# One sliding-window transformer block on one core: the unread output of the row maximum goes to two one-byte tiles in turn

## The chip, the core and the metric

The kernel runs on one core of a Trainium2 chip. The metric is the device time in microseconds (us) of that core, as the median of several executions. A core has five engines with an instruction queue each: TensorE (PE in the profile, with its weight loads as PEld), VectorE (DVE), ScalarE (ACT), GpSimd (POOL) and SyncE (SP, which only issues DMAs here). Each engine works through its own queue in order, and engines wait for each other, or for themselves, by semaphores.

## What is computed

The input is a sequence of 2048 tokens with 512 features. The reference, cut to what matters:

```python
qkv = layernorm(x) @ wqkv                       # 32 heads of 16
scores = einsum("bhqd,bhkd->bhqk", q, k) * (Dh ** -0.5)
mask = (i - j >= 0) & (i - j < 256)             # causal, window of 256
p = softmax(where(mask, scores, -1e9))
h = x + (p @ v) @ wo
g, u = layernorm(h) @ w_gate, layernorm(h) @ w_up
h2 = h + (sigmoid(g) * u) @ w_down              # inner width 1376
```

The softmax subtracts a maximum from each row of scores. That maximum is where the change lies.

## The kernel before, in words

Large products are made from pairs of 16-bit halves: a float32 operand is split into a high and a low part, and three products of parts are summed in PSUM (`mm3`, L399 to L402). The tokens go through in 8 blocks of 256 (`NB`, `B`). For a block, these pieces of work exist:

- `do_ln`: layer norm and transposition of two groups of 128 tokens.
- `do_qk` and `do_v`: the products for queries, keys and values (L402 on TensorE), whose results ScalarE and VectorE split and store (L656 on VectorE writes the low parts).
- `do_keys` and `do_queries`: DMAs that put keys and queries where TensorE reads them.
- `do_s` (L707 to L736): the scores in the layout with queries on partitions, only for the row maximum. For each of 8 groups of 4 heads there are 8 steps. A step makes 320 columns of scores with one or two matmuls (L735) into one of three PSUM tiles of the ring `s`, and queues a `row_max`.
- `row_max` (L713 to L724): one VectorE instruction (L720) that adds the mask to the scores and reduces them to the row maximum. The maximum goes to one column of the tile `mq`, through a second, short instruction that reads VectorE's accumulator. The elementwise sum has to be written somewhere too, and goes to the tile `junk`, which nobody reads. The PSUM tile is free for TensorE again when this has run (`plan.free("s", ...)`).
- `do_m`: turns 32 columns of maxima into two 16-bit halves and brings them, by DMA, into extra rows of the queries, so that the next product subtracts them.
- `do_st` (L756 to L803): the scores again, transposed (keys on partitions), with the maximum subtracted by the product itself; ScalarE takes the exponential out of PSUM (L765); GpSimd zeroes what lies outside of the window (L773, L778).
- `do_pv` (L807 to L839): probabilities times values (L826); ScalarE or VectorE takes the high half out of PSUM and VectorE the low half (L838).
- `do_o`, `do_wo`: transposition by DMA, division by the row sum (L868, L870), the output product and the residual sum.

After the last block the gated part runs in eight groups of 256 tokens: products with the gate and up weights (L1131), sigmoid and product (L1197 to L1215), and the down product (L1308, L1314). It needs no row maxima. The weights for it are prepared, by ScalarE, VectorE and GpSimd, while the attention blocks run.

The order of all this is fixed ahead of time. Each piece is a Python generator that says at every `yield` which engine it needs, for how long by the planner's estimate, and which earlier pieces must have been issued; a long list of numbers (`ORDER`) says which piece is issued next. So each engine's queue is the same list of instructions whatever the times on the chip are. For a row maximum the planner's estimate is (320 - c0) / 960 + 0.077, which is 0.41 us for 320 columns (L715). The semaphore waits are not written in the kernel; they are put in by the tile framework, from which tile each instruction reads and writes. The pool `swork`, in which `junk` lies, is opened with `reuse_waits="tile"` (L427): a new tile that takes the place of an older one waits until the instructions on that older one are done. `junk` has `bufs=1`, so each row maximum's `junk` takes the place of the one before it.

There are 8 blocks of 8 groups of 8 steps, so 512 row maxima; in the first block the four widths are 64, 128, 192 and 256 columns (`c0 = 256 - 64 * i`), 16 of each; the other 448 are over 320 columns.

Of the kernel before, what the change touches and what calls it, by code (L numbers as in the profile page):

```python
# [28 lines left out]
BF16 = mybir.dt.bfloat16  # L29
# [6 lines left out]
P = 128  # L36
# [296 lines left out]
def tile_block(ctx, tc, x, wqkv, wo, wg, wu, wd, out):  # L333
# [37 lines left out]
    def psum_tile(ring, shape, dt=F32):  # L371
        return psum.tile(shape, dt, name=ring + "p", tag=ring, bufs=RINGS[ring])
# [54 lines left out]
    swork = right.enter_context(tc.tile_pool(name="swork", bufs=2, side="right", reuse_waits="tile"))  # L427
# [279 lines left out]
    def do_s(b, g, prio):  # L707

        p, hf = g // 2, g // 4
        needs = [("queries", b, p), ("filled", 0)] + [("keys", a, hf) for a in (b, b - 1) if a >= 0]  # L710
        left = 8

        def row_max(ps, c0, x, i, e, n):  # L713
            nonlocal left
            e, = yield {DVE_: (320 - c0) / 960 + 0.077}, [e]  # L715
            plan.free("s", n, e)
            junk = swork.tile([P, 320], BF16, name="junk", bufs=1)
            if (b, hf) not in mq:
                mq[b, hf] = swork.tile([P, 8, 4], F32, name="mq", bufs=4)
            V.tensor_tensor_reduce(out=junk[:, c0:], in0=ps[:, c0:], in1=mask[:, c0:], scale=1.0, scalar=-3.0e38,  # L720
                                   op0=ALU.add, op1=ALU.max, accum_out=mq[b, hf][:, x, i:i + 1])
            left -= 1
            if left == 0:
                plan.mark(("s", b, g), e)  # L724

        for jj in range(2):
            j = 2 * (g % 2) + jj
            for i in range(4):
                c0 = 0 if b else 256 - 64 * i
                e, n = yield {PE_: (320 - c0) / 2400 + 0.006}, needs, ["s"], 0.75  # L730
                ps = psum_tile("s", [P, 320])
                q = SQ[b % 2][0:96, 4 * p + j, i].rearrange("p u t -> p (u t)")
                for a, k0, k1, col in ((b - 1, 64 * i, 256, 0), (b, 0, 64 * i + 64, 256 - 64 * i)):
                    if a >= 0:
                        PE.matmul(ps[:, col:col + k1 - k0], q, SK[0:96, (2 * a + hf) % 5, 4 * (p % 2) + j, k0:k1], start=True, stop=True)  # L735
                plan.add(prio + (4 * jj + i) / 8, row_max(ps, c0, 4 * (p % 2) + j, i, e, n))  # L736
# [745 lines left out]
```

## Time and profile before

| What | Value |
|---|---|
| time, three executions | 852.44, 852.42, 850.45 us; median 852.42 |
| profiled execution | 851.43 us, span of its instructions 849.6 us |
| TensorE busy | 765.7 us (90% of the span), 7014 matmuls |
| VectorE busy | 725.9 us (85%), 2052 instructions |
| ScalarE busy | 438.2 us (52%) |
| GpSimd busy | 277.9 us (33%) |
| mean granted TensorE clock | 0.97 |

The span runs from the first to the last instruction of the profiled execution; 1.8 us of its time lie around it. An engine is busy while at least one of its instructions is recorded as running. Records of one engine overlap: an instruction's record ends when its results are written, and the next one's can begin before that. So a record's length is not the pace at which such instructions follow each other; the pace is read from the starts. A row of the profile's groups names the line, the engine, the operation, the tiles written and read, the shape, the count, and then the busy time, the mean nanoseconds of one, and the engine's idle time ahead of them with what ended it. In the chain of waits and in the timelines the first two numbers of a row are the start, in us from the span's start, and the length.

### The profile page before, as it was taken

How to read it: one execution, taken by the hardware profiler on the slowest of the kernel's cores; microseconds unless marked ns; L12 is line 12 of the kernel's file. 1: busy time of each engine (PE TensorE's matmuls, PEld its weight loads, DVE VectorE, ACT ScalarE, POOL GpSimd, SP SyncE). 2: the span in 40 equal slices, each digit the busy share in tenths (PEclk: the TensorE clock that was granted, in tenths of full speed). 3: DMA queues.
4: the chain of work that ended last, by engine and by line, in shares of the span. 5: the costliest groups of instructions: out<-in, count | busy, mean ns of one | idle time of the engine just before them, and what ended most of it. 6: DMA issues, size and time to landing. Idle time of an engine off the chain costs nothing.

```text
span 849.6 us, 19062 instructions
## 1 busy us (share of the span) xinstructions
PE 765.7 (90%) x7014; PEld 509.9 (60%) x7014; DVE 725.9 (85%) x2052; ACT 438.2 (52%) x771; POOL 277.9 (33%) x342
## 2 busy tenths in 40 slices
PE   4788889999898899898999999658999999999997
PEld 3475557667666567566665555234756657567466
DVE  8988878888888889888987756999999888898983
ACT  5663656766568777767765766654221222112210
POOL 2632333424335354454445545655000000000000
PEclk9999988999999999999988999979999999999999
DMA  9585353374357459554965764974656458365536
GB/s 320 177 236 143 104 135 97 69 175 95 72 152 186 100 130 217 160 136 103 241 169 129 158 120 110 286 164 110 117 107 131 78 97 171 76 117 79 99 69 172
DMA packets 213326, 119.10 MB, mean 140 GB/s; under 512 B 176688, under 2 KB 185904, under 8 KB 213232
## 3 DMA queue, kind: packets, MB, share of 16 engines
q1 hardware_dynamic: 213232, 117.88, 59.1%
q8 instruction: 55, 0.90, 0.5%
q14 instruction: 39, 0.32, 0.1%
HBM read 43.65 MB, written 19.40 MB: 74 GB/s over the span
## 4 chain that ended last, share of the span: by engine, by line
PE 51%; DVE 32%; issue 7%; DMA 6%; ACT 1%; POOL 1%; DVEq 1%; SPq 0%; ACTq 0%; POOLq 0%
DVE junk L720 17%; PE sp L1131 12%; PE mmp L402 9%; PE mmp L1308 8%; PE pvp L826 6%; PE stp L1131 5%; PE sp L735 4%; PE pvp L1131 2%; PE stp L800 2%; PE stp L790 1%; DVE WD L951 1%; DMA x<-hl 1%; DVE sq L656 1%; PE mmp L1314 1%; DVE W L1021 1%
## 5 line engine op out<-in xcount | busy, mean ns | idle before, releaser
L720 DVE CUSTOM_DVE_ANT_0 junk<-sp,mask 128x320 bf16<-128x320 f32 (+4 forms) x512 | 239.5, 468 | 56.5 <-PE sp L735 9.3
L765 ACT ACTIVATE pa<-stp,kappa 128x512 f32<-128x512 f32 (+1 forms) x256 | 158.5, 645 | 81.5 <-PE stp L791 77.9
L735 PE MATMUL sp<-SK,SQ 96*128 96x256 f16 (+3 forms) x960 | 146.5, 237 | 37.3 <-DVE mq L720 29.1
L1131 PEld LDWEIGHTS <-x 128*128 128x128 f16 x1008 | 98.6, 98 | 105.9 <-issue 19.1
L1131 PE MATMUL sp<-W,x 128*128 128x512 f16 (+1 forms) x612 | 135.1, 361 | 14.2 <-DVE SQ L1154 10.5
L735 PEld LDWEIGHTS <-SQ 96*128 96x128 f16 x960 | 86.9, 99 | 86.9 <-issue 63.9
L402 PE MATMUL mmp<-xT,W 128*128 128x256 f16 x768 | 112.1, 276 | 4.9 <-DVE xT L357 2.2
L765 ACT ACTIVATE pb<-stp,kappa 128x512 f32<-128x512 f32 x128 | 85.6, 685 | 39.0 <-PE stp L800 38.1
L773 POOL TENSOR_SCALAR_AFFINE_SELECT pa<-pa 128x1024 f32<-128x1024 f32 x56 | 63.4, 1134 | 71.0 <-ACT pa L765 65.7
L402 PEld LDWEIGHTS <-W 128*128 128x128 f16 x768 | 70.3, 98 | 19.4 <-issue 5.0
L778 POOL TENSOR_SCALAR_AFFINE_SELECT pb<-pb 128x512 f32<-128x512 f32 x64 | 42.7, 667 | 71.4 <-ACT pb L765 64.2
L778 POOL TENSOR_SCALAR_AFFINE_SELECT pa<-pa 128x512 f32<-128x512 f32 x64 | 43.3, 677 | 65.3 <-ACT pa L765 65.3
L826 PE MATMUL pvp<-pa,VT 128*17 128x128 f32 (+1 forms) x1408 | 63.8, 312 | 0.6 <-DVE RH L838 0.6
L558 POOL TENSOR_TENSOR rs<-rs,nhalf 128x1 f32<-128x1 f32 x32 | 19.7, 619 | 131.5 <-DVE rs L555 131.2
L790 PE MATMUL stp<-SQ,SK 100*128 100x256 f16 x224 | 61.3, 278 | 0.0
L402 PE MATMUL mmp<-WO,oT 128*128 128x512 f16 x192 | 54.5, 405 | 5.5 <-DMA oT<-whl 5.3
L1131 PE MATMUL stp<-W,x 128*128 128x512 f16 (+1 forms) x264 | 58.2, 357 | 0.9 <-DVE SQ L359 0.6
L791 PE MATMUL stp<-SQ,SK 100*128 100x128 f16 x256 | 57.0, 223 | 0.2
L362 DVE TENSOR_TENSOR hr<-SQ,hr 128x512 f16<-128x512 f32 (+3 forms) x90 | 52.0, 588 | 2.4 <-ACT hr L355 1.6
L826 PEld LDWEIGHTS pvp<-pa,VT 128*17 128x17 f32 x1408 | 38.5, 99 | 24.7 <-issue 6.0
L800 PE MATMUL stp<-SQ,SK 100*128 100x256 f16 x256 | 50.5, 283 | 2.2 <-ACT pa L765 2.2
L1197 ACT ACTIVATE SQ<-sp,cg 128x512 f32<-128x512 f32 (+1 forms) x22 | 14.0, 638 | 73.2 <-PE sp L1131 73.2
(210 smaller groups left out, 1418.0 us busy)
## 6 DMA issues: line engine op xcount, KB each, us to landing
SQ<-sq SPq DMA_DIRECT2D x96, 128.0 KB
wr<-chunk SPq DMA_DIRECT2D x28, 256.0 KB
W<-wr SPq DMA_DIRECT2D x14, 512.0 KB
SK<-mem SPq DMA_DIRECT2D x16, 384.0 KB
chunk<-in_wd_dram SPq DMA_DIRECT2D x20, 256.0 KB
X<-in_x_dram SPq DMA_DIRECT2D x16, 256.0 KB
mem<-sk SPq DMA_DIRECT2D x8, 512.0 KB
out_dram<-X SPq DMA_DIRECT2D x16, 256.0 KB
```

What stands on the lines that cost most here:

```text
L402: PE.matmul(ps, a_of(a, k), b_of(b, k), start=(k == 0 and i == 0), stop=(k == n - 1 and i == 2))
L720: V.tensor_tensor_reduce(out=junk[:, c0:], in0=ps[:, c0:], in1=mask[:, c0:], scale=1.0, scalar=-3.0e38, op0=ALU.add, op1=ALU.max, accum_ou ...
L735: PE.matmul(ps[:, col:col + k1 - k0], q, SK[0:96, (2 * a + hf) % 5, 4 * (p % 2) + j, k0:k1], start=True, stop=True)
L765: S.activation(dst, a, AF.Exp, scale=kappa)
L773: G.affine_select(out=f, in_=f, pattern=[[0, 8], [-1, 128]], compare_op=ALU.is_gt, fill=0.0, base=0, channel_multiplier=1)
L778: G.affine_select(out=p, in_=p, pattern=[[0, 4], [1, 128]], compare_op=ALU.is_ge, fill=0.0, base=0, channel_multiplier=-1)
L790: PE.matmul(a[:, 128:384], ks(k0 + 1, g, j), qs(b, g, j, 0, 256), start=True, stop=True)
L791: PE.matmul(a[:, 384:512], ks(k0 + 3, g, j), qs(b, g, j, 128, 256), start=True, stop=True)
L800: PE.matmul(a[:, u, :], ks(k0 + 2, g, j + u), qs(b, g, j + u, 0, 256), start=True, stop=True)
L826: PE.matmul(ps[32 * j:32 * j + 17, u, q0:q1], VT[:, kt % 6, 8 * j + g, :], w[:, j, c:c + q1 - q0], start=first, stop=last, skip_group_chec ...
L1131: PE.matmul(ps, X2[p % 2][part][:, (a * COUNT[part] + at) * 2 + k, :], W[c][:, b, j, k, :], start=first and k == 0 and i == 0, stop=k == 1 ...
L1308: PE.matmul(ps, hT[p, c, r][:, a, half * kinds[c] + i, :], W["d"][2 * c + i][:, b, j, :], start=fresh and c == 0 and i == 0 and n == 0, st ...
```

## The change

The tile for the unread elementwise result becomes one byte wide per element in place of two, and there are two such tiles in turn in place of one. Two tiles of 320 bytes take as many bytes of a partition, 640, as the one tile of 320 bf16 elements did. The instruction, its inputs, its maximum and its place in VectorE's queue stay.

```diff
         def row_max(ps, c0, x, i, e, n):
             nonlocal left
             e, = yield {DVE_: (320 - c0) / 960 + 0.077}, [e]
             plan.free("s", n, e)
-            junk = swork.tile([P, 320], BF16, name="junk", bufs=1)
+            junk = swork.tile([P, 320], mybir.dt.uint8, name="junk", bufs=2)
             if (b, hf) not in mq:
                 mq[b, hf] = swork.tile([P, 8, 4], F32, name="mq", bufs=4)
             V.tensor_tensor_reduce(out=junk[:, c0:], in0=ps[:, c0:], in1=mask[:, c0:], scale=1.0, scalar=-3.0e38,
                                    op0=ALU.add, op1=ALU.max, accum_out=mq[b, hf][:, x, i:i + 1])
```

## The prediction

> **What bounds the kernel now.** I first cut the span where the row maxima begin and end, and read the busy time of each engine per stretch. The columns are the stretch and its length, then busy us and instruction count of PE, PEld, DVE, ACT and POOL, the granted clock, the DMA share and GB/s.
>
> ```profile
> core 0: us, PE busy (x) PEld busy (x) DVE busy (x) ACT busy (x) POOL busy (x), PEclk, DMA share, GB/s
> 0.00:45.40 45.40, 29.49 (x206) 20.24 (x207) 39.98 (x93) 27.48 (x54) 21.35 (x34) 0.96 0.76 252
> 45.40:483.20 437.80, 396.42 (x4446) 278.03 (x4445) 376.35 (x1316) 294.52 (x513) 186.52 (x229) 0.96 0.58 140
> 483.20:550.00 66.80, 58.41 (x515) 30.34 (x514) 47.35 (x85) 43.04 (x73) 35.30 (x39) 0.97 0.70 178
> 550.00:849.60 299.60, 281.35 (x1851) 181.27 (x1849) 262.27 (x563) 73.19 (x134) 34.71 (x41) 0.98 0.57 115
> ```
>
> Only the second stretch, 437.80 us long, holds row maxima, so only it can change directly. By busy time TensorE (396.42) stands ahead of VectorE (376.35). That is misleading, and the groups of this stretch show why:
>
> ```profile
> line engine op names shapes xcount | busy us, mean ns | idle before us <-releasers
> L720 DVE CUSTOM_DVE_ANT_0 junk<-sp,mask 128x320 bf16<-128x320 f32 (+4 forms) x512 | 239.5, 468 | 56.5 <-PE sp L735 9.3 <-PE stp L791 1.0
> L735 PE MATMUL sp<-SK,SQ 96*128 96x256 f16 (+3 forms) x958 | 146.3, 237 | 37.3 <-DVE mq L720 29.1
> L402 PE MATMUL mmp<-xT,W 128*128 128x256 f16 x638 | 95.3, 274 | 1.5 <-DVE sq L656 1.5
> L720 DVE DVE_READ_ACCUMULATOR2_ANT mq<- 128x1 f32 x512 | 42.2, 83 | 0.0
> ```
>
> VectorE is idle for 437.80 - 376.35 = 61.5 us of the stretch, and 56.5 of these lie directly before row maxima. TensorE accounts for only 9.3 + 1.0 us of them. The other 56.5 - 10.3 = 46.2 us have no releaser named. TensorE's largest idle time, 37.3 us before the score matmuls, is mostly (29.1) a wait for the row maximum. So here VectorE sets the pace, and part of its time goes to something that is neither work nor another engine. Its timeline shows what:
>
> ```profile
> start us, us, engine line op out<-in xcount [idle before <-releaser]
> 203.18 0.08 DVE L720 DVE_READ_ACCUMULATOR2_ANT mq<- 128x1 f32 x1
> 203.18 1.38 DVE L656 SCALAR_TENSOR_TENSOR sq<-mmp,sq 64x512 f16<-64x512 f32 x2
> 204.60 0.49 DVE L720 CUSTOM_DVE_ANT_0 junk<-sp,mask 128x320 bf16<-128x320 f32 x1
> 205.01 0.08 DVE L720 DVE_READ_ACCUMULATOR2_ANT mq<- 128x1 f32 x1
> 205.13 0.49 DVE L720 CUSTOM_DVE_ANT_0 junk<-sp,mask 128x320 bf16<-128x320 f32 x1
> 205.55 0.08 DVE L720 DVE_READ_ACCUMULATOR2_ANT mq<- 128x1 f32 x1
> 205.66 0.49 DVE L720 CUSTOM_DVE_ANT_0 junk<-sp,mask 128x320 bf16<-128x320 f32 x1
> 206.08 0.08 DVE L720 DVE_READ_ACCUMULATOR2_ANT mq<- 128x1 f32 x1
> 206.08 1.38 DVE L656 SCALAR_TENSOR_TENSOR sq<-mmp,sq 64x512 f16<-64x512 f32 x2
> 207.50 0.49 DVE L720 CUSTOM_DVE_ANT_0 junk<-sp,mask 128x320 bf16<-128x320 f32 x1
> 207.91 0.08 DVE L720 DVE_READ_ACCUMULATOR2_ANT mq<- 128x1 f32 x1
> 208.14 0.49 DVE L720 CUSTOM_DVE_ANT_0 junk<-sp,mask 128x320 bf16<-128x320 f32 x1
> ```
>
> Compare the starts. Behind the row maximum of 205.66 comes an L656 that touches no `junk`: it starts at 206.08, 0.42 us later, together with the accumulator read and before the row maximum's own record has ended. Behind the row maxima of 204.60, 205.13 and 207.50 comes another row maximum: 0.53, 0.53 and 0.64 us later, after the accumulator read has ended. The chain of waits has the 0.64 pair in pieces:
>
> ```profile
> 207.50 0.49 DVE junk L720
> 207.99 0.02 DVE mq L720
> 208.01 0.03 issue
> 208.04 0.02 DVEq L720
> 208.06 0.08 issue
> 208.14 0.49 DVE junk L720
> ```
>
> DVEq is VectorE's queue at work on an instruction that only waits. It can act once the accumulator read has ended (207.99 + 0.02), and the row maximum begins 0.13 us after that. I read the wait as VectorE's wait for itself. In the code the new `junk` takes the place of the last one (`bufs=1`), and the write into it must be behind the earlier write. The other output is no reason: the columns of `mq` are distinct, and the two L656 in one row (x2, 1.38 us together) write different parts of one tile directly behind each other without a gap.
>
> **The change part by part.**
>
> *Two tiles in turn.* The wait stays in the program but aims at the row maximum before the last. That one's accumulator read is over at the latest about 0.1 us into the last one (205.01 + 0.08 = 205.09 against the start at 205.13), so the wait passes while the last one runs. What a row maximum behind a row maximum then costs, no row shows, since all wait today. Bounds: with nothing left it follows after 0.42 us, as L656 does; if it has to let the accumulator read end, after 0.49 (205.01 + 0.08 - 204.60). I take 0.42, the pace of the row that stands in the same place.
>
> How many pairs? At 0.64 the idle time is 208.14 - (207.91 + 0.08) = 0.15, so the 46.2 us make about 46.2 / 0.15 = 308 pairs. Pairs at 0.53 have only some 0.03 idle each; they are left out of the count, and each would add 0.11. Per pair two things go: the 0.15 of idle time and the 0.083 of the accumulator read, which lies uncovered today. Together 46.2 + 308 x 0.083 = 46.2 + 25.6 = **71.8 us of VectorE time**. With 0.49 it is the 46.2 alone.
>
> *One byte per element.* No instruction of the trace writes single bytes, so its cost is bounded by rows on output width and on width of the tile.
>
> ```profile
> L359 DVE TENSOR_SCALAR SQ<-sp 128x512 f32<-128x512 f32 x11 | 7.6, 687 | 7.3 <-PE sp L1131 7.3
> L359 DVE TENSOR_SCALAR RH<-pvp 128x512 f16<-128x512 f32 x8 | 5.5, 686 | 5.5 <-PE pvp L826 5.5
> L720 DVE CUSTOM_DVE_ANT_0 junk<-sp,mask 128x320 bf16<-128x320 f32 x448 | 218.8, 488 | 50.3 <-PE sp L735 9.0 <-PE stp L791 1.0
> L720 DVE CUSTOM_DVE_ANT_0 junk<-sp,mask 128x64 bf16<-128x64 f32 x16 | 3.6, 223 | 1.6 <-PE sp L735 0.3
> ```
>
> From PSUM, four-byte and two-byte results take 687 and 686 ns: the width of the result does not count there. I take nothing, the value of these nearest rows. A row maximum costs (488 - 223) / 256 = 1.04 ns per element; that another 1.04 ns could be needed to place a byte is my bad end, and none of these rows points below nothing. The tiles take the bytes of the old one, so nothing else moves.
>
> *What VectorE's gain is worth.* If all else could follow, the stretch would shrink by 71.8 us. It can't quite. VectorE's busy time falls to 376.35 - 25.6 = 350.8, below TensorE's. Of TensorE's 396.42 part is only the tail of records, as this row of the chain shows beside L402's mean of 274 ns:
>
> ```profile
> 41.50 3.67 PE mmp L402 x33
> ```
>
> 33 matmuls in 3.67 us are 0.11 us each, so a record outlives the stream by some 0.16, once for each run of matmuls. TensorE's need is below 396 by an amount I can't read off; taken at face value it limits the gain to 437.8 - 396.4 = 41 us. So the ends are 41 and 72 us. Between them I go by the last stretch, without row maxima, where TensorE and VectorE feed each other in the same way: TensorE is busy 281.35 / 299.60 = 0.94 and VectorE 262.27 / 299.60 = 0.875 of it. VectorE's 350.8 at 0.94 makes 373 us (gain 65), at 0.875 401 us (gain 37). I take the middle, 387 us, a gain of **51 us**. That the queue order was laid out with 0.41 us per row maximum (L715), which is the new pace, speaks against the lower end. What is late next is TensorE, with the score matmuls in a queue between projections and `do_pv`; behind it the DMA transpositions and POOL's masking, which have the same lengths in less time. DMA is at 0.58 in the stretch and would be near 0.66.
>
> The other stretches keep their length and start earlier. Sum: 851.4 (this profiled execution; its span 849.6 and 1.8 around it) - 51 = 800.4. The median of the runs shown is 1.0 above the profiled execution, so I say **801 us**.
>
> **The rivals.**
>
> *A. Another engine or a DMA takes over early (slightly faster).* The row maxima come sooner, but TensorE has no scores ready, or the chain runs through transpositions and masks. For: TensorE's 396.4 busy us; the chain also passes DMAs and TensorE. Against: VectorE waits for TensorE before row maxima only 10.3 us in all. A gain of 5 to 20 us: some 840 us.
>
> *B. Single bytes are slow to write (slower).* Price: 1.04 ns more per element. The elements are 448 x 320 + 16 x (64 + 128 + 192 + 256) = 153,600, so 159 us more of VectorE, against 72 less: 852 + 159 - 72 = 939 us. It decides from 72 / 153.6 = 0.47 ns per element on, so from a record of 488 + 320 x 0.47 = 638 ns for 320 columns. Against: the equal 686 and 687. For: no row shows single bytes.
>
> *C. The wait is not `junk`'s, or taking it away frees nothing (the same).* The pace between row maxima might come from VectorE having to empty itself before the next such instruction. Then the gaps stay and the time is 852. Against: L656 starts 0.42 us after a row maximum. For: no row has two row maxima without a wait. The Trainium skill, "VectorE: DVE Perf Modes", section "The DRAIN you can't avoid", states such a rule: the next operation can't issue until the pipe is empty, and of eight copies with a semaphore after each and eight with one at the end it says that "the semaphore costs nothing extra here". By that rule the result is this rival's 852; the trace disagrees, with 0.42 us without and 0.53 to 0.64 with a wait behind equal instructions.
>
> **How the numbers follow.** Forecast (faster by 20 to 77 us, with the 0.49 case in it): 0.79. A: 0.07. B: 0.09. C: 0.05. So faster by over 0.3% 0.86, within 0.3% 0.05, slower by over 0.3% 0.09; 0.3% is about what a measurement of this kernel can tell from no change. The range: below, the whole 72 us and some 50 pairs at 0.53 on top (5 us), 775; above, 0.49 in place of 0.42 with its loss in coupling (46 x 51 / 72 = 33 us, so 819) and 13 us more of such loss, 832. It leaves out B, C and A, together 0.21.
>
> **What would show it.** Starts of row maxima in a row 0.42 us apart, and the unnamed idle time before L720 down from 46 to some few us (C: unchanged; the 0.49 case: the accumulator read still uncovered). A row maximum's record still near 488 ns (B: towards 820). The stretch of the row maxima some 387 us long, with VectorE's named waits for TensorE well over 10.3 us and TensorE's wait for the row maximum under 29.1; the last stretch still about 300 us. If the first two hold and the stretch is over 420 us, A is right and my share of 0.91 was wrong.

## The result and the profile after

The changed kernel takes 787.72 us (median of 4 executions, 786.26 to 790.29) against 852.18 us for the kernel before (median of 4): a ratio of 0.925, with a 95% interval of 0.922 to 0.928, so 64 us less. The profiled execution took 786.26 us, its span is 784.5 us.

First the same cut as before the change, with the stretch that holds the row maxima in the second row. The columns are the stretch and its length, busy us and count of PE, PEld, DVE, ACT and POOL, the granted clock, the DMA share and GB/s.

```profile
core 0: us, PE busy (x) PEld busy (x) DVE busy (x) ACT busy (x) POOL busy (x), PEclk, DMA share, GB/s
0.00:46.50 46.50, 29.54 (x206) 20.98 (x207) 40.05 (x92) 27.41 (x54) 21.51 (x34) 0.96 0.80 242
46.50:418.80 372.30, 361.93 (x4449) 268.37 (x4447) 351.30 (x1316) 289.72 (x514) 185.34 (x228) 1.00 0.71 165
418.80:490.00 71.20, 61.40 (x531) 31.34 (x529) 53.03 (x93) 46.59 (x81) 39.83 (x44) 0.98 0.75 193
490.00:784.50 294.50, 277.32 (x1835) 179.60 (x1833) 256.95 (x556) 69.38 (x126) 31.36 (x38) 0.99 0.56 111
```

The stretch went from 437.80 to 372.30 us, 65.5 us less. What lies behind it takes 71.2 + 294.5 = 365.7 us, against 66.8 + 299.6 = 366.4 before. So all of the gain is in the stretch. VectorE's busy time there fell from 376.35 to 351.30, and TensorE's busy share of the stretch rose from 0.91 to 361.93 / 372.30 = 0.97.

The groups of that stretch for the row maximum and the score matmuls (busy us, mean ns, then idle time before them by releaser):

```profile
L720 DVE CUSTOM_DVE_ANT_0 junk<-sp,mask 128x320 uint8<-128x320 f32 (+4 forms) x512 | 214.0, 464 | 12.1 <-PE sp L735 10.6
L735 PE MATMUL sp<-SK,SQ 96*128 96x256 f16 (+3 forms) x958 | 132.8, 232 | 5.8 <-DVE mq L720 4.0
```

The idle time before the row maxima is 12.1 us, of which 10.6 are waits for TensorE: 1.5 us have no releaser named, where there were 46.2. TensorE's wait for the row maximum fell from 29.1 to 4.0 us. VectorE's timeline shows the new pace:

```profile
start us, us, engine line op out<-in xcount [idle before <-releaser]
183.42 0.48 DVE L720 CUSTOM_DVE_ANT_0 junk<-sp,mask 128x320 uint8<-128x320 f32 x1
183.82 0.09 DVE L720 DVE_READ_ACCUMULATOR2_ANT mq<- 128x1 f32 x1
183.82 0.49 DVE L720 CUSTOM_DVE_ANT_0 junk<-sp,mask 128x320 uint8<-128x320 f32 x1
184.24 0.08 DVE L720 DVE_READ_ACCUMULATOR2_ANT mq<- 128x1 f32 x1
184.24 0.49 DVE L720 CUSTOM_DVE_ANT_0 junk<-sp,mask 128x320 uint8<-128x320 f32 x1
184.65 0.08 DVE L720 DVE_READ_ACCUMULATOR2_ANT mq<- 128x1 f32 x1
184.65 0.52 DVE L369 TENSOR_REDUCE amu<-chunk 128x1 f32<-128x352 f32 x1
```

Three row maxima start at 183.42, 183.82 and 184.24: 0.40 and 0.42 us apart, where 0.53 or 0.64 stood. Each begins together with the accumulator read of the one before, inside of the earlier record, just as the L369 at the end does. Counted over the whole stretch, a row maximum over 320 columns is followed by another one 317 times. Before the change 267 of these pairs start 0.60 to 0.65 us apart and 33 start 0.52 to 0.54 us apart; after it 276 start 0.40 to 0.43 us apart. The narrow ones of the first block follow the same line: where nothing holds it up, the next starts some 0.15 us after one of 64 columns, 0.22 after 128, 0.28 after 192 and 0.35 after 256.

### The profile page after: what moved, and what is told of

The parts are those of the page before. It is cut to its first block, busy times and chain, and to the rows that moved or that the text cites. A ratio compares the mean times of both kernels' runs of the same rounds, so it can differ in the third digit from the quotient of the medians.

```text
span 784.5 us, 19024 instructions
## 1 busy us (share of the span) xinstructions
PE 730.2 (93%) x7014; PEld 500.3 (64%) x7014; DVE 701.3 (89%) x2052; ACT 433.1 (55%) x771; POOL 278.0 (35%) x342
## 5 line engine op out<-in xcount | busy, mean ns | idle before, releaser
L720 DVE CUSTOM_DVE_ANT_0 junk<-sp,mask 128x320 uint8<-128x320 f32 (+4 forms) x512 | 214.0, 464 | 12.1 <-PE sp L735 10.6
L765 ACT ACTIVATE pa<-stp,kappa 128x512 f32<-128x512 f32 (+1 forms) x256 | 156.4, 645 | 48.3 <-PE stp L791 45.4
L735 PE MATMUL sp<-SK,SQ 96*128 96x256 f16 (+3 forms) x960 | 133.0, 232 | 5.8 <-DVE mq L720 4.0
L735 PEld LDWEIGHTS <-SQ 96*128 96x128 f16 x960 | 81.7, 97 | 37.1 <-issue 14.2
L765 ACT ACTIVATE pb<-stp,kappa 128x512 f32<-128x512 f32 x128 | 85.2, 686 | 19.5 <-PE stp L800 17.8
L790 PE MATMUL stp<-SQ,SK 100*128 100x256 f16 x224 | 59.6, 271 | 0.0
L402 PE MATMUL mmp<-WO,oT 128*128 128x512 f16 x192 | 51.7, 389 | 5.5 <-DMA oT<-whl 5.1
L791 PE MATMUL stp<-SQ,SK 100*128 100x128 f16 x256 | 55.6, 218 | 0.1
L789 PE MATMUL stp<-SQ,SK 100*128 100x128 f16 x224 | 49.3, 220 | 1.5 <-DMA SQ<-mt 0.7
```

What stands on the lines that cost most here:

```text
L402: PE.matmul(ps, a_of(a, k), b_of(b, k), start=(k == 0 and i == 0), stop=(k == n - 1 and i == 2))
L765: S.activation(dst, a, AF.Exp, scale=kappa)
L790: PE.matmul(a[:, 128:384], ks(k0 + 1, g, j), qs(b, g, j, 0, 256), start=True, stop=True)
L791: PE.matmul(a[:, 384:512], ks(k0 + 3, g, j), qs(b, g, j, 128, 256), start=True, stop=True)
```

## The experiments

The theory: the gain is VectorE's wait for its own last write into `junk`, and the second tile alone takes it away. The rivals: single bytes are quicker (or slower) to write; and the gain is not a sum over row maxima, but came with TensorE's clock or another chain. The first three runs tell these apart. The other five ask what limits the stretch before and after, which the prediction had only guessed at. Each ratio below is to runs of the kernel before on the same chip; their median was 850.31 us for the runs with two tiles, with single bytes, with half of the blocks and with the narrow row maximum after the change, and 851.62 us for the other four. The diffs are against the changed kernel, except where both kernels are named. In kernels with an added line, L721 and L736 are what L720 and L735 are in the others.

### Two tiles, without the single bytes

Two tiles of bf16 take 1280 bytes of a partition in place of 640; to make room, `mq` and `mt` have fewer buffers.

```diff
-            junk = swork.tile([P, 320], mybir.dt.uint8, name="junk", bufs=2)
+            junk = swork.tile([P, 320], BF16, name="junk", bufs=2)
...
-                mq[b, hf] = swork.tile([P, 8, 4], F32, name="mq", bufs=4)
+                mq[b, hf] = swork.tile([P, 8, 4], F32, name="mq", bufs=2)
...
-        mt = swork.tile([P, 1, P], F16, name="mt")
+        mt = swork.tile([P, 1, P], F16, name="mt", bufs=1)
```

> Two tiles in turn, but of bf16 as before; to make room mq has two buffers in place of four and mt one in place of two. If the gain comes from the second tile alone, this runs like the changed kernel: 788 us, at most 5 us more for the shrunk mq and mt. If single bytes are themselves quicker to write (rival), it lies between, at 800 us or more.

Measured: 788.17 us, ratio 0.928 (0.926 to 0.931). The group of row maxima over 320 columns in this run:

```profile
L720 DVE CUSTOM_DVE_ANT_0 junk<-sp,mask 128x320 bf16<-128x320 f32 x448 | 196.3, 484 | 10.9 <-PE sp L735 9.6
```

The ratio is near the 0.925 of the changed kernel, with intervals that overlap; the stretch of the row maxima is 372.9 us long, against 372.3. And a record of two-byte results takes the same 484 ns as the next row of the changed kernel shows for single bytes:

```profile
L720 DVE CUSTOM_DVE_ANT_0 junk<-sp,mask 128x320 uint8<-128x320 f32 x448 | 196.1, 484 | 10.4 <-PE sp L735 9.3
```

The second tile is enough.

### Single bytes, without the second tile

```diff
-            junk = swork.tile([P, 320], mybir.dt.uint8, name="junk", bufs=2)
+            junk = swork.tile([P, 320], mybir.dt.uint8, name="junk", bufs=1)
```

> Single bytes, but one tile. If the gain comes from the second tile alone: 852 us as before, row maxima in a row 0.53 and 0.64 us apart, records near 488 ns. If single bytes are quicker (rival): clearly under 852 us, up to the whole 65 us, with shorter records.

Measured: 849.12 us, ratio 0.999 (0.998 to 1.001). Its group:

```profile
L720 DVE CUSTOM_DVE_ANT_0 junk<-sp,mask 128x320 uint8<-128x320 f32 x448 | 218.5, 488 | 49.7 <-PE sp L735 8.5 <-PE stp L791 1.0
```

488 ns and 49.7 us of idle time, as before the change (488 and 50.3). The pairs of row maxima also start as they did: 267 of 317 are 0.60 to 0.65 us apart and 33 are 0.52 to 0.54. The width of the result costs and gains nothing; in the change it only lets two tiles fit in the bytes of one.

### Two tiles in half of the blocks

```diff
+    junks = [swork.tile([P, 320], mybir.dt.uint8, name=f"junk{i}", bufs=1) for i in range(2)]
...
-            junk = swork.tile([P, 320], mybir.dt.uint8, name="junk", bufs=2)
+            junk = junks[left % 2 if b >= 4 else 0]
```

> One byte-wide tile for blocks 0 to 3, two in turn for blocks 4 to 7. If the gain is a sum over pairs of row maxima, the first half stays at some 201 us and the second at some 206: 823 us (788 + 35). If TensorE's fuller clock or a late chain makes the gain (rival), it is lost as a whole or kept as a whole: 788 to 800 or 845 to 852 us.

Measured: 823.67 us, ratio 0.971 (0.968 to 0.975). The two halves of the stretch, cut at the first row maximum of block 4, and the row maxima in each:

```profile
46.50:248.50 202.00, 181.87 (x1958) 129.17 (x1956) 170.70 (x642) 124.72 (x234) 70.90 (x89) 0.96 0.50 129
248.50:455.10 206.60, 199.31 (x2492) 144.71 (x2492) 195.75 (x674) 167.35 (x281) 115.01 (x140) 1.00 0.75 171
```

```profile
L721 DVE CUSTOM_DVE_ANT_0 junk<-sp,mask 128x320 uint8<-128x320 f32 (+4 forms) x256 | 114.3, 446 | 29.9 <-PE sp L736 6.2
```

```profile
L721 DVE CUSTOM_DVE_ANT_0 junk<-sp,mask 128x320 uint8<-128x320 f32 x256 | 113.6, 484 | 6.3 <-PE sp L736 2.9
```

In the kernel before, the same two halves are:

```profile
45.40:246.50 201.10, 180.67 (x1958) 128.61 (x1957) 170.82 (x643) 124.52 (x234) 70.91 (x89) 0.97 0.51 129
246.50:483.20 236.70, 215.75 (x2490) 149.42 (x2489) 205.53 (x674) 170.00 (x280) 115.61 (x140) 0.96 0.64 150
```

The half with one tile takes 202 us, about as long as before, with 29.9 us of idle time before row maxima; the half with two takes 206.6 where it took 236.7, with 6.3 us of idle time. The gain is a sum over places, not a state that the whole kernel falls into. In the second half 17 of 177 pairs still start 0.63 to 0.65 us apart. A likely reason is that `left % 2` alternates within a group only, so that neighbours from two groups can get the same tile; this was not looked into.

### VectorE's work cut, before and after the change

```diff
+            c0 += 64 if c0 == 0 else 0
             V.tensor_tensor_reduce(out=junk[:, c0:], in0=ps[:, c0:], in1=mask[:, c0:], scale=1.0, scalar=-3.0e38,
```

In the kernel before:

> The kernel before, but row maxima over 320 columns leave out the first 64 (a maximum over fewer keys): 30 us less of VectorE. If VectorE set the pace alone before: 821 to 826 us. If the pace was shared with TensorE: 832 to 842 us.

Measured: 826.43 us, ratio 0.970 (0.968 to 0.972), 0.4 us above the range for VectorE alone. In the changed kernel:

> The changed kernel, but row maxima over 320 columns leave out the first 64, so the maximum is over fewer keys. That is 448 x 64 x 1.04 ns = 30 us less of VectorE. If VectorE still sets the pace alone after the change: 758 to 763 us. If TensorE and VectorE now limit each other: 770 to 780 us. If VectorE no longer counts: 785 to 788 us.

Measured: 786.85 us, ratio 0.925 (0.922 to 0.928), the same as the changed kernel. The stretches of the two runs, the kernel before first:

```profile
46.00:458.50 412.50, 385.08 (x4448) 274.95 (x4447) 348.88 (x1316) 292.14 (x513) 184.90 (x229) 0.98 0.63 149
```

```profile
45.50:416.40 370.90, 360.26 (x4446) 267.88 (x4443) 330.69 (x1316) 288.51 (x513) 184.27 (x227) 1.00 0.72 165
```

Before the change a cut of 30 us of VectorE work, 27.5 us by its busy time (376.35 to 348.88), brings 25 us. After it 20.6 us less busy time on VectorE (351.30 to 330.69) bring 1.4 us of the stretch. VectorE is idle for 19.2 us more, and 12.7 of these show in its wait for the scores, which was 10.6 us in the changed kernel and is 23.3 in the second run:

```profile
DVE junk L720 <- PE sp L735: 10.6, 29, 0.9
```

```profile
DVE junk L721 <- PE sp L736: 23.3, 54, 1.3
```

VectorE mostly waits for scores instead: after the change a faster VectorE runs into TensorE.

### TensorE's work cut, before and after the change

```diff
-                mm3(ps[:, j, :], lambda a, k: W1[:, a, k, c0:c0 + P], lambda a, k: xT[b][:, a, k, :], k, KT)
+                for i, (h, l) in enumerate(((0, 0), (0, 1))):
+                    PE.matmul(ps[:, j, :], W1[:, h, k, c0:c0 + P], xT[b][:, l, k, :], start=(k == 0 and i == 0), stop=(k == KT - 1 and i == 1))
```

In the kernel before:

> The kernel before with the same third product left out. If VectorE set the pace before: 846 to 852 us, 28 us of TensorE gone for next to nothing. If TensorE had a share: 825 to 840 us.

Measured: 852.27 us, ratio 1.001 (0.999 to 1.003), 0.3 us above the range for VectorE. In the changed kernel:

> The changed kernel, but the query and key products leave out the third of their three partial products (high weights times high tokens and high times low stay): 256 matmuls of 256 columns less, 0.11 us each, 28 us of TensorE, of which some 638/768 = 24 us lie beside row maxima. If TensorE now sets the pace: 760 to 768 us. If it is TensorE and VectorE by turns: 770 to 780 us. If ScalarE, GpSimd or DMAs set it: 784 to 788 us.

Measured: 788.21 us (784.81 to 790.58), ratio 0.924 (0.922 to 0.926), as the changed kernel. The stretches, the kernel before first:

```profile
45.70:484.30 438.60, 384.84 (x4238) 259.85 (x4236) 378.57 (x1316) 292.46 (x511) 185.90 (x229) 0.95 0.58 140
```

```profile
45.80:420.40 374.60, 350.73 (x4236) 250.01 (x4234) 353.22 (x1316) 286.70 (x512) 185.75 (x228) 1.00 0.71 164
```

Before the change, TensorE's work is free: some 28 us of it less change nothing. That VectorE set the pace is so shown from both sides: 25 of 30 us came through on VectorE, none of 28 on TensorE. After the change I had expected 760 to 768 us if TensorE sets the pace, and that was wrong: TensorE alone doesn't set it either. Its wait for the row maximum, 4.0 us in the changed kernel, took up a part of what was cut, 6.7 us:

```profile
PE sp L736 <- DVE mq L721: 10.7, 17, 2.0
```

The range that the time came out at, 784 to 788, I had put down to ScalarE, GpSimd or DMAs. One more run separates that from a balance of two.

### Both cuts in the changed kernel

> The changed kernel with both cuts: row maxima without the first 64 columns and query and key products without the third partial product. If TensorE set the pace after the change and VectorE is right behind it, the narrow row maximum, worth about 1 us alone, is worth 8 us or more on top of the shorter products. If VectorE is well clear, it stays within 3 us of the changed kernel with the shorter products alone.

Measured: 777.42 us (776.56 to 782.70), ratio 0.914 (0.911 to 0.917); 10 us under the changed kernel, and 10.8 us under the one with the shorter products alone, where the expectation asked for 8 or more.

```profile
44.30:407.90 363.60, 344.91 (x4232) 247.76 (x4230) 328.81 (x1317) 285.23 (x512) 186.23 (x227) 1.00 0.73 168
```

Either cut alone brings nothing, both together bring 10 us. So after the change TensorE and VectorE are about level, and each holds the stretch where it is when the other gets faster. They are not the only limit: the cuts are worth some 24 and 30 us, and 10 came out. VectorE's busy share falls to 328.81 / 363.60 = 0.90. What holds the rest, ScalarE's and GpSimd's turns, DMA transpositions, or the two engines' fixed order, was not tried and stays open.

## Why the prediction was right, and where its size was off

**What bounds the kernel.** Right: the run with TensorE's work cut (1.001) and the run with VectorE's work cut (25 of 30 us) show that VectorE set the pace, though TensorE had the larger busy time. The 46.2 us without a releaser were VectorE's wait for itself: they are gone with two tiles of either width, and there with one tile of either width. The argument that the other output, `mq`, is no reason rested on a weak row: the two L656 behind each other show no gap, but also no overlap. The second starts at 203.87, 0.69 us after the first and at the end of its record, while an L656 behind a row maximum starts 0.07 us before that record ends. So they did not show that nothing held the second one up. The runs settle it: between the one with a single byte-wide tile and the changed kernel only the number of `junk` tiles differs, and with it the waits are there or gone.

**Two tiles in turn.** Right in mechanism and size. The pace of 0.42 us, taken from the row of another instruction behind a row maximum, held: 0.40 to 0.42, and 0.40 to 0.43 in 276 of 317 pairs. The other end, 0.49, with the accumulator read still uncovered, fell: the next row maximum starts with the read. Forecast were 46.2 us of idle time and 25.6 of uncovered reads, 71.8 together. Measured are 46.2 - 1.5 = 44.7 and 376.35 - 351.30 = 25.1, together 69.8. The count of 308 pairs was near too: 267 pairs of 320 columns and 39 narrower ones were held up by some 0.23 us each before the change, 306 in all, and 40 were held up by about 0.11.

**One byte per element.** Right: nothing. Rival B needed 638 ns per record and got 484, the same as two-byte results with two tiles.

**Rival C** fell with the 0.40 to 0.42 between row maxima that nothing holds up. So the rule that the prediction quoted from the Trainium skill ("VectorE: DVE Perf Modes", "The DRAIN you can't avoid"), that a semaphore costs nothing extra here, doesn't hold for a wait on the row maximum directly in front: in this kernel each cost 0.11 to 0.23 us, and the single-tile run (ratio 0.999) beside the two-tile runs (0.925 and 0.928) is that cost in the whole. The same section also says, which the prediction left out, that a next operation which isn't held starts earlier. The pace of 0.41 us beside a record of 484 ns agrees with that.

**What VectorE's gain is worth.** This is the term that was mis-sized. Of the 71.8 us I let 51 come through; 65.5 did. The loss to waiting elsewhere was to be 21 us and was 4: VectorE's other idle time in the stretch was 61.5 - 46.2 = 15.3 us before and is (372.30 - 351.30) - 1.5 = 19.5 us after. I had taken VectorE's busy share from the last stretch and gone for the middle of what 0.875 and 0.94 give, which was a choice and not a derivation. It became 351.30 / 372.30 = 0.944, the upper end, for which the prediction had worked out 373 us. The last stretch was a poor stand-in: the shares of these two engines at other work say little about how two queues fit together here. The limit of 41 us from TensorE's busy time taken at face value was wrong as a limit, as suspected: with the same matmuls that busy time fell from 396.42 to 361.93, 34.5 us less. It counts the tails of records, one for each gap, and gaps closed: TensorE's idle time in the stretch went from 41.4 to 10.4 us. The higher granted clock (0.96 to 1.00) has a share in it as well, by an estimate at most 0.04 x 396 = 16 us; the two were not taken apart. So before the change this busy time bounded nothing. TensorE came next, as forecast, but not alone: VectorE is level with it.

**Rival A** (a gain of 5 to 20 us) did not come about; the named waits of VectorE for TensorE stayed at 10.6 us, where I had expected well over 10.3.

## What to carry to other kernels

An output that nobody reads still makes its next writer wait when it has one buffer; idle time of the same small size before most instances of one instruction, with no other engine named, is the sign of it, and the pace of an unrelated instruction behind the same one tells what the wait costs. A busy time that contains record tails is no lower bound on what an engine needs: cut its work in an experiment and see whether the time follows. And when neither of two cuts alone moves the time, make both before blaming a third engine.

## What was not expected of the hardware

TensorE's granted clock rose with the change: 0.96 in the stretch before, 1.00 after. This is not an even slowing. Cut into pieces of 5 us, the stretch before shows 0.99 or 1.00 in 77 of 88 pieces and 0.50 to 0.84 in the other eleven, four of them in a row from 115 to 135 us (0.58, 0.74, 0.60, 0.71); the stretch after shows 1.00 in every piece. In the 5 us ahead of 115 TensorE was busy for 3.44 us, one of its lowest values; but from 390 to 395 us it was busy for 3.11 and the clock stayed at 1.00, so the busy share of one such piece doesn't tell when the clock drops. In the run with two tiles in half of the blocks it is 0.96 in the half with one tile and 1.00 in the other, so that run doesn't part the clock from the gain; with TensorE's work cut in the kernel before it is lowest, 0.95, and that run lost no time by it (1.001). So the clock went along with the gain and was not shown to be a cause. A few us of the gain are not excluded: of the 13 executions of the kernel before that belong to the first four runs, the shortest, 847.29 us, has a clock of 0.980 over its span, and one of 851.11 us has 0.967. The Trainium skill, "TensorE: Matmul & The Clock Gate", section "Part 1: The HAM clock gate (the "warmup" mystery)", says that the gate lets fewer pulses through according to how busy TensorE has been of late. A fuller TensorE with a clock of 1.00 agrees with that in direction; no run here shows the rule itself.
